# Batch 0's keys and queries of head pairs 2 and 3 transposed at their landing, ahead of the scores and values of pair 1

## The chip, the cores and the metric

The kernel runs on one core of one Trainium2 chip. Times are device microseconds (us) of that core. Runs of the kernel before differ by 0.4 to 0.9 us within one set of rounds; for each comparison the kernel before was run on the same chip in the same rounds. All runs here count as fast in the sense of the run's state. The *granted clock* is the share of full TensorE clock that the throttle granted, averaged over a run or a stretch. A load *lands* when its transfer is complete. A profiled span is 1.8 us shorter than the time of the same run.

## The reference, cut to what matters

Chunked attention over 4 batches, 8 heads, 768 positions, 64 wide: each chunk of 32 queries sees 16 positions to its left, 8 to its right and 8 memory slots. Its output goes through a two-layer block with a sine:

```python
scores = scale * np.matmul(q_c, k_full.transpose(0, 1, 3, 2))
a = softmax(scores)                       # cut: with the maximum taken off
out[:, :, c_start:c_end] = np.matmul(a, v_full)
# ...
h = x @ w_in                              # 3072 x 512 by 512 x 2048
s = np.sin(alpha * h)
g = h + s * s / (alpha + 1e-09)
return g @ w_out
```

## The kernel before: the parts that matter

Batch 0's attention runs alone, before the first layer has anything to do. Eight *units* are worked off: unit u is head pair u // 2 and four of its eight query blocks. The order of the pieces is written by hand: k and q transpose a pair's keys or queries (TensorE) and evict them (DVE for keys, ACT for queries, DVE for pair 1's queries), s makes a unit's scores, e its exponentials on ACT, v its values, x the transposes of its output, z n multiplies zeros n times so that TensorE stays busy.

```python
ORDER = (
    "k 0,q 0,memk 0,memv 0,k 1,s 0,e 0,z 1,s 1,e 1,q 1,s 2,e 2,v 0,s 3,e 3,k 2,x 0,q 2,v 1,s 4,e 4,k 3,x 1,q 3,"
    "s 5,e 5,v 2,z 1,s 6,e 6,x 2,v 3,z 1,s 7,e 7,x 3,z 1,v 4,z 1,v 5,x 4,z 1,v 6,x 5,z 1,v 7,x 6,z 1,x 7"
)
# ... accumulators: "big" has three of two banks, "sm" two of one bank
big = ctx.enter_context(tc.tile_pool(name="big", bufs=3, space=bass.MemoryType.PSUM))
smp = ctx.enter_context(tc.tile_pool(name="smp", bufs=2, space=bass.MemoryType.PSUM))
# ... the loads of batch 0, in the order in which they are asked for
load_qk_pair(0, 0, *kq)
masks.make_identity(nc, ident[:])
load_qk_pair(0, 1, *kq)
load_v(0, 0, 16)
for hp in range(2, HP):
    load_qk_pair(0, hp, *kq)
# ... in turn(), the transposes of one pair
            spin(3 if hp < 2 else 2, z)           # fillers in front of them
# ... in exps()
                nc.scalar.activation(pt[...], sc[...], ACTF.Exp, bias=..., scale=0.125)   # cut
# ... in pv() and xt()
        ot = big.tile([P, 2, 512], F32, name="ot", tag="big")     # values of a unit
        nc.vector.reciprocal(rv, otv[0:QW, :, :, D])
        nc.vector.tensor_tensor(out=x_blk[...], in0=otv[...], in1=rv[...], op=ALU.mult)   # cut
```

The softmax here doesn't subtract the row's maximum and nothing guards it: scores larger than these inputs give would overflow.

## Time and profile before

| | |
|---|---|
| time, median | 234.26 us (233.97 to 234.29) |
| profiled span | 232.5 us |
| first layer starts | 28.00 us |
| rest of the span behind that | 204.5 us |

Only the 28 us of batch 0's attention are reordered. A start of layer one that is x us earlier is worth x us, if the other 204.5 us keep their length. The lines are in the prediction.

### The profile page before, as it was taken

To read this page: it belongs to the slowest core of one execution; us is meant where nothing else is said; L and a number is where in the kernel's file an instruction comes from. 1 tells how busy PE (TensorE), PEld (TensorE's weight loads), DVE (VectorE), ACT (ScalarE), POOL (GpSimd) and SP (SyncE) were. 2 spreads that over 40 slices of the span, in tenths; PEclk is the share of its full clock that TensorE was granted. 3 is DMA by queue.
4 is the path that set the end of the run, shared out by engine and by line. 5 is a ranking of instruction groups with operands and counts; after the bars stand their busy time and mean duration, and the time that the engine had idled before them with its cause. 6 is when DMAs were issued, how large, how long until landed. Compare 5 with 4: busy or idle time off the path is not lost.

```text
span 232.5 us, 4584 instructions
## 1 busy us (share of the span) xinstructions
PE 218.9 (94%) x1834; PEld 122.1 (53%) x1834; DVE 160.2 (69%) x287; ACT 153.0 (66%) x247; POOL 69.8 (30%) x80
## 2 busy tenths in 40 slices
PE   7978899999999999999999999998999999899994
PEld 2444555555446565654555656564555555453453
DVE  5776679898657887988467798887565458775110
ACT  3388779984797397898564877878664676880110
POOL 8898202595912115157300315020000020110000
PEclk9999999999999999999999999999999999999999
DMA  6999999999999910109993101010111010101112
GB/s 88 142 173 169 207 204 206 207 139 99 138 239 164 91 45 0 43 8 174 171 156 80 45 0 48 0 45 3 45 48 53 37 49 0 45 1 48 69 67 90
DMA packets 51805, 21.13 MB, mean 91 GB/s; under 512 B 36296, under 2 KB 48840, under 8 KB 51784
## 3 DMA queue, kind: packets, MB, share of 16 engines
q0 software_dynamic: 45568, 14.41, 70.3%
q1 hardware_dynamic: 6216, 6.43, 9.2%
q8 instruction: 14, 0.23, 0.5%
q14 instruction: 7, 0.06, 0.1%
HBM read 28.94 MB, written 6.29 MB: 152 GB/s over the span
## 4 chain that ended last, share of the span: by engine, by line
PE 66%; ACT 11%; DVE 11%; issue 5%; DMA 3%; POOL 2%; POOLq 1%; DVEq 0%; ACTq 0%
PE o L472 28%; PE hT L393 21%; DVE gT L422 5%; ACT u L405 4%; PE ot L301 3%; PE sc L270 3%; DMA k_bf<-in_k_dram 3%; ACT pt L286 2%; PE ot L316 2%; DVE x_blk L306 2%; DVE s L414 2%; ACT s L408 2%; PE tt_a L242 2%; PE o L461 2%; PE z L162 1%
## 5 line engine op out<-in xcount | busy, mean ns | idle before, releaser
L472 PE MATMUL o<-w_out_sb,gT 128*128 128x512 bf16 x336 | 90.0, 380 | 0.4 <-DVE gT L422 0.4
L393 PE MATMUL hT<-xT,w_in_sb 128*128 128x384 bf16 x488 | 87.1, 326 | 2.9 <-DVE gT L422 2.8
L422 DVE SCALAR_TENSOR_TENSOR gT<-s,inv_alpha,hT 128x768 bf16<-128x768 f32 x61 | 61.0, 1012 | 19.7 <-ACT s L408 11.6
L405 ACT ACTIVATE u<-hT,alpha_sb 128x768 f32<-128x768 f32 x61 | 54.7, 897 | 23.9 <-PE hT L393 22.9
L393 PEld LDWEIGHTS <-w_in_sb 128*128 128x128 bf16 x512 | 49.3, 98 | 37.5 <-issue 3.8
L286 ACT ACTIVATE pt<-sc,biasm 128x256 bf16<-128x256 f32 (+2 forms) x104 | 39.0, 471 | 14.6 <-PE sc L270 14.6
L472 PEld LDWEIGHTS <-gT 128*128 128x128 bf16 x336 | 29.3, 98 | 24.3 <-DVE gT L422 1.2
L410 POOL TENSOR_TENSOR s<-u 128x768 f32<-128x768 f32 x9 | 13.2, 1465 | 88.2 <-ACT u L405 61.3
L408 ACT ACTIVATE s<-u 128x768 f32<-128x768 f32 x32 | 27.0, 843 | 1.0
L414 DVE TENSOR_TENSOR s<-u 128x768 f32<-128x768 f32 x23 | 24.3, 1056 | 3.1 <-ACT u L405 3.0
L306 DVE TENSOR_TENSOR x_blk<-ot,rinv 96x512 bf16<-96x512 f32 x32 | 22.0, 686 | 1.1
L139 POOL DMA_DIRECT2D vw<-in_v_dram x24 | 22.0, 938 | 0.0
L216 POOL COPY pr<-q_bf 128x768 bf16<-128x768 bf16 x12 | 10.7, 895 | 35.7 <-PE tt_a L242 25.0
L430 DVE COPY o_sb<-o 128x512 f32<-128x512 f32 x12 | 8.3, 689 | 15.6 <-PE o L472 15.5
L430 ACT COPY o_sb<-o 128x512 f32<-128x512 f32 x11 | 6.4, 582 | 17.9 <-PE o L472 17.9
L305 DVE RECIPROCAL rinv<-ot 96x8 f32<-96x8 f32 x32 | 6.5, 202 | 16.2 <-PE ot L301 15.8
L301 PEld LDWEIGHTS <-pt 128*128 128x128 bf16 x256 | 11.8, 97 | 6.4 <-issue 1.5
L270 PEld LDWEIGHTS <-kTi 64*128 64x128 bf16 x256 | 6.9, 94 | 13.3 <-issue 6.0
L301 PE MATMUL ot<-vw,pt 128*128 128x65 bf16 x256 | 13.0, 193 | 0.6 <-ACT pt L286 0.6
L270 PE MATMUL sc<-qT,kTi 64*128 64x96 bf16 x256 | 11.2, 205 | 2.4 <-DVE qT L263 1.1
L242 PEld LDWEIGHTS <-pr 128*128 128x128 bf16 x144 | 10.0, 98 | 5.9 <-DVE pr L216 0.9
L316 PE MATMUL ot<-ident,x_blk 96*128 96x96 bf16 x128 | 10.8, 206 | 2.0 <-DVE x_blk L306 2.0
(74 smaller groups left out, 168.1 us busy)
## 6 DMA issues: line engine op xcount, KB each, us to landing
out_dram<-o_sb SPq DMA_DIRECT2D x23, 256.0 KB, 2.0
k_bf<-in_k_dram POOLq DMA_DIRECT2D x3, 768.0 KB, 7.4
q_bf<-in_q_dram POOLq DMA_DIRECT2D x3, 768.0 KB, 12.0
vw<-in_v_dram POOLq DMA_DIRECT2D x6, 384.0 KB, 14.1
w_in_sb<-in_moe_w_in_dram POOLq DMA_DIRECT2D x4, 512.0 KB, 10.1
w_out_sb<-in_moe_w_out_dram POOLq DMA_DIRECT2D x2, 1024.0 KB, 24.5
k_bf<-in_k_dram POOLq DMA_DIRECT2D x4, 192.0 KB, 5.4
q_bf<-in_q_dram POOLq DMA_DIRECT2D x4, 192.0 KB, 5.5
```

What stands on the lines that cost most here:

```text
L139: nc.gpsimd.dma_start(dst, src)
L270: nc.tensor.matmul(sc[:, e, QW * c:QW * c + QW], kTi[64 * e:64 * e + 64, hp, 104 * j:104 * j + P], qT[64 * e:64 * e + 64, hp, QW * j:QW * ...
L286: nc.scalar.activation(pt[:, 0:H * QW].rearrange("p (g e c) -> p e g c", g=4, e=2)[:, :, c0:c1, 32 * m:32 * m + 32], sc[:, :, 0:4 * QW].re ...
L301: nc.tensor.matmul(otv[:, n // 4, n % 4, :], pt[:, QW * n:QW * n + P], vws[b % 2][:, 2 * hp + n % 2, j, 0:D + 1])
L306: nc.vector.tensor_tensor(out=x_blk[:].rearrange("p (g e) d -> p g e d", g=2), in0=otv[0:QW, :, :, 0:D], in1=rv.unsqueeze(3).to_broadcast( ...
L316: nc.tensor.transpose(xtp[:, kt, :], x_blk[:, 2 * kt:2 * kt + 2, :].rearrange("p e d -> p (e d)"), ident[0:QW, 0:QW])
L393: nc.tensor.matmul(hts[hf][:, 0:HALF], w_in_sb[:, kt, P * ft:P * ft + P], xT[:, kt, HALF * hf:HALF * hf + HALF], start=(kt == 0), stop=(kt ...
L405: nc.scalar.activation(u[:], hT[:, :, 0:HALF], ACTF.Sin, scale=alpha_sb[:, ft:ft + 1])
L408: nc.scalar.activation(s2[:], u[:], ACTF.Square)
L414: nc.vector.tensor_tensor(out=s2[:], in0=u[:], in1=u[:], op=ALU.mult)
L422: nc.vector.scalar_tensor_tensor(out=gv, in0=s2[:], scalar=inv_alpha[:, ft:ft + 1], in1=hT[:, :, 0:HALF], op0=ALU.mult, op1=ALU.add)
L472: nc.tensor.matmul(o[:], gT[:, ft, P * s:P * s + P], w_out_sb[:, ft, :], start=(ft == 0), stop=(ft == FT - 1),)
```

## The change

Its intent: pairs 2 and 3 are transposed as soon as their loads land, so that ACT need not wait for them later. The fillers ahead of the four turns become 3, 3, 1, 1 and no longer 2 each.

```diff
-    "k 0,q 0,memk 0,memv 0,k 1,s 0,e 0,z 1,s 1,e 1,q 1,s 2,e 2,v 0,s 3,e 3,k 2,x 0,q 2,v 1,s 4,e 4,k 3,x 1,q 3,"
+    "k 0,q 0,memk 0,memv 0,k 1,s 0,e 0,z 1,s 1,e 1,q 1,k 2,s 2,e 2,s 3,v 0,q 2,e 3,k 3,x 0,v 1,q 3,s 4,e 4,x 1,"
     "s 5,e 5,v 2,z 1,s 6,e 6,x 2,v 3,z 1,s 7,e 7,x 3,z 1,v 4,z 1,v 5,x 4,z 1,v 6,x 5,z 1,v 7,x 6,z 1,x 7"
@@
-            spin(3 if hp < 2 else 2, z)
+            spin(3 if hp < 2 else (3 - 2 * (hp - 2)), z)
```

## The prediction

> **What bounds the kernel now.** The span by stage comes first. This is the table of busy times in four stretches; the columns are the stretch in us, its length, the busy time and instruction count of PE, PEld, DVE, ACT and POOL, the granted clock, the DMA share and GB/s.
>
> ```profile
> 10.00:14.00 4.00, 2.94 (x59) 1.71 (x56) 2.83 (x6) 2.98 (x10) 4.00 (x6) 1.00 1.51 187
> 14.00:20.00 6.00, 5.46 (x97) 3.13 (x94) 4.45 (x12) 4.56 (x13) 6.00 (x9) 1.00 2.33 150
> 20.00:28.00 8.00, 5.80 (x98) 3.78 (x97) 6.12 (x16) 7.15 (x18) 3.98 (x5) 1.00 1.29 200
> 28.00:52.00 24.00, 22.98 (x144) 13.41 (x142) 19.82 (x23) 20.59 (x28) 10.27 (x10) 1.00 1.31 190
> ```
>
> The change edits only the order of batch 0's attention, which runs up to 28.0 us; the other 204.5 us keep their instructions and their order. So the change can be worth only what it takes off the moment at which the first layer's matmuls start. In 20 to 28 us ACT is the busiest (7.15 of 8.00); in 14 to 20 us ACT is busy for 4.56 of 6.00 and PE for 5.46, but part of the latter is the filler multiplications of zeros. The next view, ACT in order of time, shows where ACT stood still. "pt<-sc" is the exponentials of units of four cells, four instructions each; "qT<-z" is the eviction of a pair's transposed queries.
>
> ```profile
> 10.41 2.60 ACT L286 ACTIVATE pt<-sc,biasm 128x64 bf16<-128x64 f32 x8 [1.46 <-PE sc L270]
> 13.62 2.60 ACT L286 ACTIVATE pt<-sc,biasm 128x64 bf16<-128x64 f32 x8 [0.61 <-PE sc L270]
> 16.40 0.80 ACT L263 COPY qT<-z 128x768 bf16<-128x768 bf16 x1 [0.19 <-PE z L245]
> 17.64 1.35 ACT L286 ACTIVATE pt<-sc,biasm 128x64 bf16<-128x64 f32 x4 [0.44 <-PE sc L270]
> 19.80 0.80 ACT L263 COPY qT<-z 128x768 bf16<-128x768 bf16 x1 [0.81 <-PE z L245]
> 20.50 3.85 ACT L286 ACTIVATE pt<-sc,biasm 128x256 bf16<-128x256 f32 x12
> 24.36 1.28 ACT L369 ACT_TABLE_LOAD   x1
> ```
>
> Units 2 and 3 run from 13.62, unit 4 at 17.64, units 5 to 7 from 20.50 without a gap. Between 13.62 and 20.50 ACT stood idle for 0.19 + 0.44 + 0.81 = 1.44 us, each time for something made from the keys or queries of pairs 2 and 3, which were transposed late. The chain of work that ended last says that this idle time is paid for (start, duration, what):
>
> ```profile
> 18.87 0.43 PE z L162 x2
> 19.30 0.47 PE z L245 x12
> 19.80 0.80 ACT qT L263
> 20.60 1.26 ACT pt L286 x4
> 21.86 0.04 issue
> 21.91 0.42 PE ot L301 x8
> 22.32 0.02 issue
> 22.35 0.21 DVE rinv L305
> ```
>
> It goes from the transposes of pair 3's queries (19.30) through their eviction and unit 5's exponentials to unit 3's values at 21.91. Those values do not use unit 5: its exponentials hold the two-bank accumulator that unit 3's values are given, as the code's three "big" buffers in rotation show (unit 5's scores, then unit 3's values, take the same one). After 22 us the chain alternates DVE, PE and ACT to the start of layer one at 28.0.
>
> The last view is the issue of pair 2's keys, size and time from the start of issue to landing; ahead of it the queue's own line, with its start.
>
> ```profile
> 7.51 0.78 POOL L107 DMA_DIRECT2D k_bf<-in_k_dram  x1
> ```
> ```profile
> k_bf<-in_k_dram POOLq DMA_DIRECT2D x1, 192.0 KB, 5.5
> ```
>
> So pair 2's keys land at 7.51 + 5.5 = 13.0. From the same two views for the others: pair 2's queries 8.25 + 5.8 = 14.05, pair 3's keys 9.81 + 5.2 = 15.0, its queries 10.89 + 5.2 = 16.1. The kernel before transposes these at 14.67, 15.84, 18.07 and 19.23: up to 3 us after landing.
>
> **What the Trainium skill says.** "PSUM — Partial Sum Buffer", section "Engine vs sequencer instructions", calls the queues of ScalarE and VectorE strict FIFO and says that matmuls start and complete in program order. The trace agrees: the transposes of unit 0's output start at 15.13 and take 0.34, but their DVE copy starts at 16.24, behind pair 2's key copies (15.24 to 16.24). So an eviction put forward delays what stood ahead of it. "TensorE: Matmul & The Clock Gate", section "Step-by-step: what each phase is for", says that only weight loads are pulled ahead; here one weight load for unit 4's scores ran at 16.64 while its matmul waited until 17.25. So keys put in front of unit 2's scores can hold those scores, by their DMA too. "ScalarE: Activation LUTs", section "What ACT_TABLE_LOAD costs", gives about 1283 ns and a drain of 1380 ns; the load here took 1.28 us and the sine after it began at 25.66, so no such drain is seen. This load follows unit 7's exponentials and moves with them.
>
> **The change part by part.** No instruction is added or removed. Four evictions (two of 1.00 us of DVE for keys with their edges, two of 0.80 us of ACT) and 48 transposes move forward. The filler was 2 multiplications in front of each of four turns (8); it is 3, 3, 1, 1 (8). I replay the order with durations of the traced rows, as steps from one start to the next: 12 transposes 0.46 on PE (0.53 to their end), a unit's scores 0.28 and values 0.35, fillers 0.75 for three and 0.31 for one, exponentials 1.30 to 1.33, reciprocal 0.24, scaling 0.69, DVE copy of an output block 0.32; 0.04 for a hand-over.
>
> Up to the transposes of pair 1's queries (11.65 to 12.18) nothing differs.
> - *Pair 2's keys.* Three fillers end at 12.86, landing is 13.0: transposes 13.03 to 13.56. PE was waiting for the DVE copy of pair 1's queries until 13.18 anyway, so most of this is in idle time.
> - *Units 2 and 3's scores, unit 0's values.* Scores 2 at 13.49, against 13.23: 0.26 lost. Exponentials 2 run 13.88 to 15.18. Scores 3 at 13.77, values 0 at 14.05 to 14.47.
> - *DVE.* Pair 2's key copies 13.60 to 14.60, then unit 0's reciprocal and scaling to 15.53, against 14.89.
> - *Pair 2's queries.* Three fillers from 14.40, transposes 15.15 to 15.68, eviction on ACT 15.71 to 16.51. ACT waits 0.53 for it, from 15.18, because it stands in front of exponentials 3. These then run 16.51 to 17.81, against an end at 16.22.
> - *Pair 3's keys, unit 0's transposes, unit 1's values, pair 3's queries.* Keys 15.92 to 16.45; output transposes 16.38; values 1 at 16.56; one filler 16.91; queries 17.22 to 17.75. Their eviction finds ACT just free: 17.81 to 18.61.
> - *From there ACT is never idle.* Exponentials 4 run 18.61 to 19.94 (before: 17.64 to 18.99, so later); 5 to 21.26 (before 21.86), 6 to 22.55, 7 to 23.84 (before 24.35). DVE meanwhile copies pair 3's keys (16.49 to 17.49) and output 0, scales unit 1 by 18.74; output 1 is transposed at 18.78, scores 5 at 19.06, values 2 at 19.53, scores 6 at 20.18, output 2 at 20.96. All are earlier than before by 0.4 or more, or ready for ACT in time.
> - *Values 3* get their buffer at 21.26 and start at 21.31 instead of 21.91: 0.60 gained. After that the chain is the same as before. Output 4's copy waits for ACT's table load and sine; both move with unit 7's end, by 0.51.
>
> The sum, checked on ACT: idle time falls from 1.44 to 0.53 (0.91 gained), unit 2 starts 0.26 later, and about 0.1 is lost as hand-overs that overlapped: 0.5 to 0.6. Layer one starts at about 27.45. Nothing behind it should eat this: in 28 to 60 us no wait for a DMA is listed among the waits, the first quarter of the first weights lands at 17.39 + 6.7 = 24.1, and the output weights issued at 22.88 and 23.75 land at 45.3 and 50.4, the first 5 us ahead of their first use at 50.40. The second is used only after the first two accumulators' first halves.
>
> **The rivals.** First, *the moved work costs more than it frees*: DVE and ACT are FIFO, and pair 3's queries reach ACT with 0.06 us of slack only. Against it stands that each landing is ahead of its transposes except pair 2's keys. If those landed at 13.6 instead of 13.0, everything to unit 7 would move by up to 0.6 and the time would be 234.2. Second, *the gain is hidden*: the end of the stage has its own bound of DVE, PE and ACT hand-overs, busy 6.12 of 8.00 us on DVE. For it speaks that unit 4's end becomes later (19.94); against it that the chain named unit 5's exponentials as what released unit 3's values. It would give 234.2 too. Third, *a larger gain*: if PE runs its fillers and transposes faster than my steps, pair 2's queries reach ACT by 15.2, the wait of 0.53 vanishes and about 1.0 us is saved: 233.2. Against it stands that the steps are read off this same trace. Fourth, *a longer stage*: with evictions ahead of unit 0's and 1's scaling, the values of pair 1 could be held by the accumulators so that PE idles and ACT drains; I would expect 234.8. The values of pairs 2 and 3 landing at 20.0 to 22.1 do not forbid the earlier values 4 at 23.14.
>
> **Range and chances.** 234.26 - 0.55 = 233.7 us. The replay may be off by some 0.5 us in either direction (one landing, one hand-over on ACT), and the runs of before spread over 0.3: 233.0 to 234.4 should hold it 8 times in 10. Two per cent is 4.7 us; all ACT idle time in the whole reordered stretch is 1.44, so faster by over 2% is 1%, within 2% is 98%, and slower by over 2%, which would need a new wait that repeats beyond this stage, is 1%.
>
> **What would show it.** Right: scores 2 about 0.26 later behind the landing of pair 2's keys; ACT without a gap from the eviction of pair 2's queries (about 15.7) to the table load, which starts near 23.84; exponentials 4 later and 5 earlier than before; values 3 near 21.3; layer one near 27.45; all later stages shifted by one constant. Wrong: an ACT gap in front of pair 3's query eviction, values 3 still at 21.9 with another releaser, or the shift at 28 us gone by 52 us.

## The result, and the profile after

The changed kernel took 233.72 us in the median of four runs (233.18 to 234.03), the kernel before 234.12 (233.91 to 234.29). Ratios here are the mean time of one kernel's fast runs over that of the other's of the same rounds, so not quite the ratio of the medians. This one is 0.9981, with a 95% interval of 0.9957 to 1.0005. The size is near the predicted one; the interval still holds 1.

ACT after, in order of time, to be laid beside ACT before in the prediction:

```profile
15.20 0.80 ACT L263 COPY qT<-z 128x768 bf16<-128x768 bf16 x1 [0.27 <-PE z L245]
15.89 1.36 ACT L286 ACTIVATE pt<-sc,biasm 128x256 bf16<-128x256 f32 x4
...
17.86 3.85 ACT L286 ACTIVATE pt<-sc,biasm 128x64 bf16<-128x64 f32 x12
22.38 1.35 ACT L286 ACTIVATE pt<-sc,biasm 128x256 bf16<-128x256 f32 x4 [0.67 <-PE sc L270]
23.75 1.28 ACT L369 ACT_TABLE_LOAD   x1
```

Units 4 to 6 now run without a gap from 17.86, before 4 began at 17.64 and 5 only at 20.50. The two gaps that stood ahead of units 4 and 5 are gone. But unit 7 waited 0.67 us for its scores, which nobody had foreseen. PE after, around that time:

```profile
12.73 0.53 PE L245 MATMUL z<-ident,k_bf 128*64 128x128 bf16 x12 [0.27 <-DMA k_bf<-in_k_dram]
...
19.27 0.40 PE L301 MATMUL ot<-vw,pt 128*128 128x65 bf16 x8 [0.43 <-ACT pt L286]
...
20.87 0.60 PE L301 MATMUL ot<-vw,pt 128*128 128x65 bf16 x8
21.28 0.62 PE L162 MATMUL z<-zeros 128*128 128x512 bf16 x1
...
27.55 0.34 PE L316 MATMUL ot<-ident,x_blk 96*128 96x96 bf16 x4 [0.28 <-DVE x_blk L306]
```

Unit 3's values start at 20.87, 1.04 us earlier than the 21.91 of before. The last output transposes start at 27.55 (layer one at 27.73) against 27.82 before: of the 1.04, only 0.27 is left. In between the same eight value matmuls took 0.60 instead of 0.40, a filler 0.62 instead of 0.38. The busy times by stretch say why (columns as in the prediction; the third value from the end is the granted clock). First the changed kernel, then the kernel before:

```profile
20.00:22.00 2.00, 1.47 (x27) 0.86 (x23) 1.44 (x4) 1.71 (x6) 1.55 (x3) 0.73 1.36 186
22.00:24.00 2.00, 1.84 (x22) 1.16 (x19) 0.90 (x3) 1.60 (x5) 2.00 (x3) 0.50 1.26 212
24.00:26.00 2.00, 1.69 (x27) 1.25 (x26) 1.83 (x6) 1.71 (x3) 0.16 (x1) 0.92 1.23 202
```
```profile
20.00:22.00 2.00, 1.39 (x27) 0.91 (x26) 1.10 (x3) 2.00 (x7) 1.35 (x2) 1.00 1.44 179
22.00:24.00 2.00, 1.47 (x31) 0.97 (x31) 1.33 (x4) 2.00 (x8) 1.98 (x3) 1.00 1.25 207
```

The changed kernel ran at half clock for about 3.4 us, from 20.9 to 24.3, as stretches of half a us show. From 28 us on the two traces run in parallel: the first output matmul starts at 50.40 before and at 50.13 after, again 0.27 apart. So two things are mixed in the 0.4 us, a gain from the order and a loss from the clock. A third one, the landing of pair 2's keys, is in the first line above: PE waited for it, and it came at 7.51 + 5.2 = 12.7 here, where the trace before had promised 13.0.

### The profile page after: what moved, and what is told of

Its sections match the earlier page's. It is cut to its first block, busy times and chain, and to the rows that moved or that the text cites. A ratio compares the mean times of both kernels' runs of the same rounds, so it can differ in the third digit from the quotient of the medians.

```text
span 232.2 us, 4583 instructions
## 1 busy us (share of the span) xinstructions
PE 219.2 (94%) x1834; PEld 122.7 (53%) x1834; DVE 160.1 (69%) x287; ACT 153.0 (66%) x247; POOL 70.0 (30%) x80
## 4 chain that ended last, share of the span: by engine, by line
PE 64%; ACT 12%; DVE 11%; issue 5%; POOL 3%; DMA 2%; POOLq 1%; DVEq 0%; ACTq 0%
PE o L472 28%; PE hT L393 21%; DVE gT L422 5%; ACT u L405 4%; PE ot L301 3%; ACT pt L286 3%; PE sc L270 3%; DVE x_blk L306 2%; PE ot L316 2%; DMA k_bf<-in_k_dram 2%; DVE s L414 2%; ACT s L408 2%; PE tt_a L242 2%; PE o L461 2%; PE o L442 1%
## 5 line engine op out<-in xcount | busy, mean ns | idle before, releaser
L286 ACT ACTIVATE pt<-sc,biasm 128x256 bf16<-128x256 f32 (+2 forms) x104 | 39.1, 470 | 15.1 <-PE sc L270 15.1
L472 PEld LDWEIGHTS <-gT 128*128 128x128 bf16 x336 | 29.3, 98 | 24.3 <-DVE gT L422 1.2
L414 DVE TENSOR_TENSOR s<-u 128x768 f32<-128x768 f32 x23 | 24.3, 1056 | 3.1 <-ACT u L405 3.0
L301 PEld LDWEIGHTS <-pt 128*128 128x128 bf16 x256 | 12.4, 100 | 6.7 <-issue 2.2
L301 PE MATMUL ot<-vw,pt 128*128 128x65 bf16 x256 | 13.6, 197 | 0.9 <-ACT pt L286 0.9
L316 PEld LDWEIGHTS <-x_blk 96*128 96x128 bf16 x128 | 8.3, 98 | 8.4 <-DVE x_blk L306 3.8
```

The costliest lines, as they stand in the source:

```text
L286: nc.scalar.activation(pt[:, 0:H * QW].rearrange("p (g e c) -> p e g c", g=4, e=2)[:, :, c0:c1, 32 * m:32 * m + 32], sc[:, :, 0:4 * QW].re ...
L301: nc.tensor.matmul(otv[:, n // 4, n % 4, :], pt[:, QW * n:QW * n + P], vws[b % 2][:, 2 * hp + n % 2, j, 0:D + 1])
L316: nc.tensor.transpose(xtp[:, kt, :], x_blk[:, 2 * kt:2 * kt + 2, :].rearrange("p e d -> p (e d)"), ident[0:QW, 0:QW])
L414: nc.vector.tensor_tensor(out=s2[:], in0=u[:], in1=u[:], op=ALU.mult)
L472: nc.tensor.matmul(o[:], gT[:, ft, P * s:P * s + P], w_out_sb[:, ft, :], start=(ft == 0), stop=(ft == FT - 1),)
```

## The experiments

My theory by now: (1) ACT's idle time from unit 2 on sets the start of layer one; (2) the new order hangs on the landing of pair 2's keys, which varies; (3) the new order leaves TensorE so thinly busy from 17 to 21 us that the clock sometimes drops. The rivals: the filler split carries the gain; the end of the stage is set by hand-overs between PE and DVE; the clock drop is an accident that belongs to any order. All outputs are right.

To compare traces whose loads landed at different times I use one distance throughout: from the start of unit 2's scores to the start of layer one. It was 14.77 us before (13.23 to 28.00):

```profile
9.56 0.53 PE L245 MATMUL zb<-ident,k_bf 128*64 128x128 bf16 x12 [0.51 <-DMA k_bf<-in_k_dram]
...
13.23 0.34 PE L270 MATMUL sc<-qT,kTi 64*128 64x96 bf16 x8 [1.06 <-DVE qT L263]
...
28.00 1.30 PE L393 MATMUL hT<-xT,w_in_sb 128*128 128x384 bf16 x7
```

This distance leaves out what the landing of pair 2's keys costs ahead of it. For that, a second one starts at the transposes of pair 1's keys (9.56), which stand ahead of everything that was reordered: 28.00 - 9.56 = 18.44 before.

### The changed kernel again

No edit.

> The changed kernel once more, unaltered, for a second trace. Ordering theory: the ratio to the kernel before is again about 0.998 (0.3 to 0.6 us gained). Clock theory (the traced run of the changed kernel had a slower granted clock, about 0.79 in 20 to 28 us, and paid some 0.7 us for it): if the drop is the rule for this order, this trace shows it again, with unit 3's values about 1.0 us earlier than before but layer one only 0.3 earlier; if it was chance, the clock is 1.00 in 20 to 28 us and layer one starts 0.8 or more earlier than before (27.2 or less).

Six runs: 233.00 to 235.47 us, median 233.61, before 233.87 (11 runs). The ratio was 1.0007 (0.9976 to 1.0037): in this round no gain at all in the mean. The runs split by their clock. The four with a mean clock of 0.998 or more took 233.00, 233.05, 233.15 and 234.07; the two with 0.992 and 0.985 took 234.42 and 235.47. The traced run had full clock:

```profile
8.61 0.53 PE L245 MATMUL zb<-ident,k_bf 128*64 128x128 bf16 x12 [0.19 <-DMA k_bf<-in_k_dram]
...
12.35 0.53 PE L245 MATMUL z<-ident,k_bf 128*64 128x128 bf16 x12 [0.37 <-DMA k_bf<-in_k_dram]
12.80 0.51 PE L270 MATMUL sc<-qT,kTi 64*128 64x96 bf16 x16
...
19.02 0.40 PE L301 MATMUL ot<-vw,pt 128*128 128x65 bf16 x8 [0.43 <-ACT pt L286]
...
26.75 2.44 PE L393 MATMUL hT<-xT,w_in_sb 128*128 128x384 bf16 x14
```

The distance is 26.75 - 12.80 = 13.95, against 14.54 in the first trace (13.19 to 27.73): the clock drop cost 0.6 us there. The order alone is worth 14.77 - 13.95 = 0.82, less what scores 2 are held by the landing. They came 4.19 us after pair 1's keys and not 3.67 as before, so 0.52 goes back: from pair 1's keys to layer one it is 18.14 here, 0.30 less than before.

### Fillers as before, in the new order

```diff
-            spin(3 if hp < 2 else (3 - 2 * (hp - 2)), z)
+            spin(3 if hp < 2 else 2, z)
```

> New order, but the fillers as before: 2 in front of each of the four turns, not 3, 3, 1, 1. Ordering theory: pair 2's keys wait for their landing anyway, pair 2's queries reach ACT about 0.2 us earlier, pair 3's queries after that no later in ACT's row; time within 0.2 us of the changed kernel. Rival (the filler split carries the gain): the gain falls below 0.2 us.

Median 233.24 us, ratio 0.9977 (0.9959 to 0.9995). The traced distance is 13.63 (12.94 to 26.57), 0.32 shorter than with 3, 3, 1, 1. Against the changed kernel of the same rounds its median is 0.37 lower; within 0.2 had been expected. Its ACT, then its PE lines for unit 2's values and for layer one:

```profile
17.14 0.80 ACT L263 COPY qT<-z 128x768 bf16<-128x768 bf16 x1 [0.35 <-PE z L245]
...
22.94 1.28 ACT L369 ACT_TABLE_LOAD   x1
```

```profile
18.76 0.40 PE L301 MATMUL ot<-vw,pt 128*128 128x65 bf16 x8 [0.17 <-DVE xT L319]
...
26.57 2.60 PE L393 MATMUL hT<-xT,w_in_sb 128*128 128x384 bf16 x15
```

Unit 2's values wait here for the DVE copy of output 1. In the changed kernel they waited for ACT, until unit 4's exponentials ended. The waits in the two compiled programs say the same: the first matmul of these values waits for DVE in one and for ACT in the other, and unit 6's scores the other way round. So the accumulators are not given out in strict rotation; the change of fillers alone altered which one unit 2's values got, and it was the worse one. The filler split carries no gain: with it the path is 0.32 us longer. How much of this is the accumulator and how much the fillers themselves was not separated.

### The new fillers alone, in the old order

```diff
-            spin(3 if hp < 2 else 2, z)
+            spin(3 if hp < 2 else (3 - 2 * (hp - 2)), z)
```

> Old order with the new filler split (3 in front of each of pair 2's turns, 1 in front of pair 3's). Ordering theory: nothing gained, 0.995 to 1.003 of before, perhaps 0.2 us lost on pair 2's queries and won back on pair 3's, which were on the path. Rival (the fillers carry it): 0.3 to 0.6 us gained here already.

Ratio 1.0003 (0.9989 to 1.0017), traced distance 14.77 (13.01 to 27.78), as before. The rival falls.

### The gaps of PE filled

```diff
-    "... v 1,q 3,s 4,e 4,x 1,"
-    "s 5,e 5,v 2,z 1,s 6,e 6,x 2,v 3, ..."
+    "... v 1,q 3,s 4,e 4,z 2,x 1,"
+    "s 5,e 5,z 1,v 2,z 1,s 6,e 6,z 2,x 2,v 3, ..."
```

> The changed kernel with five more multiplications of zeros, put where its trace showed PE waiting between 17.6 and 20.7 us (two ahead of unit 1's output transposes, one ahead of unit 2's values, two ahead of unit 2's output transposes). Clock theory: the granted clock stays 1.00 in 20 to 28 us, layer one starts 0.4 us or more earlier than in the traced changed kernel (27.3 or less) and the time is 0.3 to 0.7 us below the changed kernel's slower runs, about 233.2. Ordering theory alone (the clock is an accident that costs nothing on the path): the same time as the changed kernel or slightly more for the added work.

No run had a mean clock under 0.998. But the median was 234.11 us, ratio 1.0009 (0.9993 to 1.0026): the expected time was missed by 0.9. Its trace shows where that run lost it:

```profile
13.85 0.53 PE L245 MATMUL z<-ident,k_bf 128*64 128x128 bf16 x12 [1.00 <-DMA k_bf<-in_k_dram]
```

Pair 2's keys landed at 13.8, 1.5 us later than in the second trace of the changed kernel, and PE waited 1.00 for them. The distance from scores 2 on is 13.80 (14.31 to 28.11), so the fillers did not lengthen the path in this trace. The load is the same program in both; in this traced run it took 6.3 us from issue to landing, in the others 4.8 to 5.6. Why all six runs of this kernel were slowish (mean 234.09, where the changed kernel's four at full clock had 233.32 in the same rounds) was not traced and stays open.

### Pair 2's keys asked for earlier

```diff
     load_qk_pair(0, 1, *kq)
+    load_qk_one(k, kq[0], 2)      # pair 2's keys
     load_v(0, 0, 16)
-    for hp in range(2, HP):
-        load_qk_pair(0, hp, *kq)
+    load_qk_one(q, kq[1], 2)
+    load_qk_pair(0, 3, *kq)
```

> The changed kernel with one load moved: pair 2's keys are asked for ahead of unit 0's and 1's values instead of behind them. So far the traces of the new order agree that layer one starts a fixed 14.1 to 14.4 us after pair 2's keys are transposed (12.35 to 26.75, 12.48 to 26.57, 13.85 to 28.11; 12.73 to 27.73 with a clock drop), so their landing, 12.3 to 13.8, would set the end of the stage. Landing theory: PE no longer waits for that DMA, scores 2 start when pair 1's queries are copied, layer one starts at 26.2 to 27.0 and the runs without a clock drop are at 232.6 to 233.1. Rival (the stage's end is set elsewhere and the fixed distance is chance): layer one stays at 26.6 to 28, times as the changed kernel's. Second rival: the values of unit 0, now 0.7 us later in the queue, become the wait.

PE no longer waits for the DMA:

```profile
12.66 0.53 PE L252 MATMUL z<-ident,k_bf 128*64 128x128 bf16 x12
...
27.14 2.12 PE L400 MATMUL hT<-xT,w_in_sb 128*128 128x384 bf16 x12
```

But the gain was not what I expected: layer one at 27.14, not 26.2 to 27.0, and 233.09, 233.36 and 233.45 us in the three runs at full clock, as the changed kernel. Scores 2, at 13.20, now wait for the DVE copy of pair 1's queries (12.19 to 13.14), and pair 1's keys are transposed at 9.37, later than the 8.6 to 9.1 of the first three traces of the new order. That the moved load made them late is not shown: with all loads in their old places they came at 9.49 in the trace with gaps filled, and with this load moved at 8.83 in the trace with the gaps filled as well. Counted from them, scores 2 came after 3.83 us, where the new order with the old loads has 4.10 to 4.82, and layer one after 17.77, where the changed kernel had 18.14. So this trace gained about 0.4 us behind pair 1's keys and lost more than that ahead of them. The last stretch, from the end of the exponentials to layer one, is 3.89 here. Three of six runs had clocks of 0.993, 0.983 and 0.978 and took 234.11, 234.91 and 235.82, which makes the ratio 1.0013 (0.998 to 1.0046).

### The same load moved, in the old order

> The old order with the same load moved. There pair 2's keys are transposed at 14.67, long after landing, and layer one started 18.44 us after pair 1's keys were transposed in both traces at hand. Landing theory: nothing gained, 0.998 to 1.003 of before, and the distance of 18.44 from pair 1's keys stands. Rival (an earlier key load speeds either order, by the queue): 0.3 us or more gained here too.

The distance is 14.76, and 18.43 from pair 1's keys, both as expected. The time was worse than expected: ratio 1.0034 (1.0013 to 1.0055), with one of four runs at a clock of 0.991. The profiled run, 234.33, has the 232.5 of the traced kernel before as its span, but it too lies above the 233.95 of before in these rounds. Why all four runs were slower is open.

### Both: keys earlier and gaps filled

> The same load moved, with the five fillers in PE's waits of 17.6 to 20.7 us as well. Clock theory: so far the mean granted clock was 0.993 or less in 5 of 16 runs of the new order, and in none of the runs of before, of the old order with new fillers, or of the new order with its gaps filled; here too no run falls below 0.997, and the spread of the times is under 0.8 us, all at 232.6 to 233.3. Rival (the five fillers themselves slow the stage, as the six slow runs of the gaps-filled kernel could also be read): 0.5 us or more above the kernel with only the load moved.

No run under 0.998, median 233.73 us, ratio 0.999 (0.9974 to 1.0006). The clock part held, the times did not: 233.14 to 234.35, wider and later than 232.6 to 233.3. The mean, 233.71, is 0.41 above the three runs at full clock of the kernel with only the load moved, near the 0.5 of the rival (the fillers themselves slow the stage). In its trace the distance is 14.18, pair 2's queries reached ACT 0.43 us late, and the values of unit 4 waited 0.21 us for a load of values. So this rival is not ruled out here.

### Pair 2's keys asked for later

The mirror image, in the kernel with two fillers everywhere: pair 2's queries are asked for first.

```diff
-    for hp in range(2, HP):
-        load_qk_pair(0, hp, *kq)
+    load_qk_one(q, kq[1], 2)
+    load_qk_one(k, kq[0], 2)
+    load_qk_pair(0, 3, *kq)
```

> The new order with two fillers everywhere, and pair 2's queries asked for ahead of its keys instead of behind them: the keys land about 0.75 us later, nothing else in the queue moves. Landing theory: PE waits for the keys 0.7 us longer than the 0.52 of the kernel with two fillers (1.2 or so), scores 2 start 0.7 us later after pair 1's keys are transposed (4.13 becomes 4.8), the distance from scores 2 to layer one stays at 13.6, and the runs without a clock drop take 233.4 to 234.0 and not 232.7 to 233.3. Rival (the landing is hidden, as it would be in the old order): scores 2 and the time as with two fillers.

Median 234.59 us, ratio 1.002 (1.0005 to 1.0035); the five runs at full clock took 234.12 to 234.87. The traced keys landed at 8.25 + 5.7 = 13.95 and PE waited:

```profile
14.02 0.53 PE L252 MATMUL z<-ident,k_bf 128*64 128x128 bf16 x12 [1.86 <-DMA k_bf<-in_k_dram]
```

From pair 1's keys to scores 2 it took 5.46 (9.02 to 14.48) instead of 4.13: 1.33 us, where I had expected 0.7. The traced run then fell to half clock (0.61 in 14 to 18 us), so its distance of 15.10 says nothing. The times say it: the five runs at full clock have a mean of 234.47, the eight of the kernel with two fillers (two sets of rounds, one below) 233.33, so 1.1 us of the 1.33 is paid; set against the kernel before of the same rounds it is 1.1 too (0.45 slower, 0.66 faster). This load lies on the path of the new order. In the old order, by its first trace, there were 1.7 us between landing and use (13.0 to 14.67).

### Pair 3's query eviction done twice

```diff
         t = turn(qb, hp)
+        if qb.shape[1] != 6 and hp == 3:
+            copy(qT[:, hp, :]..., t[...])      # the same eviction once more
         copy(qT[:, hp, :]..., t[...])
```

> The changed kernel with pair 3's query eviction done twice on ACT (0.80 us more of ACT ahead of unit 4's exponentials, same result). By the prediction ACT is the row without gaps that ends the stage: layer one 0.7 us later after pair 2's keys than the 14.1 to 14.4 us of the new order, so 14.8 to 15.1. Rival (from unit 2's values on, the end is set by hand-overs between PE and DVE and ACT has slack): less than 0.3 us later, 14.1 to 14.6.

From pair 2's keys to layer one it took 14.71 (12.64 to 27.35), between the expected 14.8 to 15.1 and the rival's 14.1 to 14.6, so by its own terms this test does not decide. The distance from scores 2 is 14.25: 0.30 more than in the changed kernel, 0.62 more than with two fillers everywhere. The second comparison is the fair one: in this build unit 2's values got the DVE-freed accumulator, as there. Its ACT:

```profile
17.08 0.80 ACT L264 COPY qT<-z 128x768 bf16<-128x768 bf16 x1
17.91 0.80 ACT L265 COPY qT<-z 128x768 bf16<-128x768 bf16 x1
18.60 5.09 ACT L288 ACTIVATE pt<-sc,biasm 128x64 bf16<-128x64 f32 x16
23.71 1.28 ACT L371 ACT_TABLE_LOAD   x1
```

The second eviction adds 0.83 us from start to start (17.08 to 17.91). The first begins 3.98 us after scores 2, 0.22 earlier than with two fillers (12.94 to 17.14), and the end moved by 0.62. What is added on ACT comes out at the end, so ACT sets the end. The time: median 234.42 us, ratio 1.0022 (0.9996 to 1.0047), with one of four runs at a clock of 0.993. The same is seen without any doubling: from the table load, that is the end of the exponentials, to layer one it takes 3.62 to 3.64 us in eight traces, old and new order alike (24.36 to 28.00 before, 22.94 to 26.57 with two fillers, 23.71 to 27.35 here). In the changed kernel at full clock it is 3.75, where unit 7 waits for its scores, and 3.89 and 3.90 in the two new-order kernels with the earlier key load; there the end is not ACT's alone.

### Only pair 2 moved

```diff
-    "... q 1,k 2,s 2,e 2,s 3,v 0,q 2,e 3,k 3,x 0,v 1,q 3,s 4,e 4,x 1,"
+    "... q 1,k 2,s 2,e 2,s 3,v 0,q 2,e 3,x 0,v 1,s 4,e 4,k 3,x 1,q 3,"
```
(with two fillers everywhere)

> One part alone: only pair 2's keys and queries are moved forward; pair 3's stay behind unit 4's exponentials as before, two fillers everywhere. By the prediction ACT then waits for pair 3's queries again: ACT idle of 0.3 to 0.8 us ahead of that eviction, and scores 2 to layer one between the old 14.77 and the new 13.6, near 14.2. Rival (pair 2 alone carries the gain): 13.6 to 13.8. Second rival (pair 3 alone): 14.7 or more.

The distance is 13.63 (13.67 to 27.30), the same as with both pairs moved. The rival was right: pair 2 alone carries the whole gain. ACT:

```profile
16.16 2.60 ACT L286 ACTIVATE pt<-sc,biasm 128x256 bf16<-128x256 f32 x8
19.10 0.80 ACT L263 COPY qT<-z 128x768 bf16<-128x768 bf16 x1 [0.34 <-PE z L245]
19.80 3.85 ACT L286 ACTIVATE pt<-sc,biasm 128x256 bf16<-128x256 f32 x12
23.66 1.28 ACT L369 ACT_TABLE_LOAD   x1
```

ACT idles 0.34 us ahead of pair 3's queries, now behind unit 4. With both pairs moved and the same fillers it idles 0.35 ahead of the same eviction, only earlier, behind unit 3. The sum of ACT's idle time behind unit 2's start is the same, and so is the end. Moving pair 2 brings scores 4 forward (2.89 us after scores 2 instead of 4.02), and pair 3 follows in its old place. Moving pair 3 as well buys nothing. Median 233.76 us, ratio 0.998 (0.9965 to 0.9995), though PE waited 1.17 for the keys in this trace; none of its six runs was under 0.998 in clock.

### Two fillers everywhere, with and without the gaps filled

> The new order with two fillers everywhere, a second time beside the one with gaps filled. Expected: scores 2 to layer one again 13.6, runs without a clock drop 232.7 to 233.4, one or two of six runs with a mean clock near 0.993 and 0.6 us or more slower. If no run drops and the times equal those of the other, the clock is not what separates fast from slow runs.

> New order, fillers 2 in front of every turn as before, and the five fillers in PE's waits: meant to beat both kernels. In the traces so far layer one starts 14.77 us after scores 2 in the old order and 13.95 in the changed kernel, but 13.63 with two fillers everywhere, because unit 2's values then take the buffer that output 1's copy frees and not the one that unit 4's exponentials hold. Buffer and clock theory: 13.6 to 13.8 here, no run with a mean clock under 0.997, 0.996 to 0.998 of before with all runs between 232.7 and 233.6. Rival (the added fillers cost more than the clock drops): at or above the kernel without them, 0.998 to 1.000.

With the gaps filled: median 233.17 us (232.82 to 233.72), before 234.17, ratio 0.9965 (0.9951 to 0.998). It is the fastest kernel of the study and clear of the kernel before. The distance was 13.64. One run, 233.72, lies above the range that I gave. Without the gaps filled: median 233.83, ratio 0.9984 (0.9969 to 0.9999), two of six runs at a clock of 0.993 (233.87 and 233.88). A slow one, 234.22, had full clock, so the clock is not the only thing that parts slow from fast runs; of the four at full clock only one (233.08) lies in the expected 232.7 to 233.4. The traced run of the kernel without was one with a drop; its distance is 14.23 (13.36 to 27.59) and not 13.63, again 0.6 us. Without, then with the gaps filled:

```profile
18.00:21.00 3.00, 1.91 (x37) 1.34 (x38) 1.59 (x5) 3.00 (x11) 3.00 (x5) 1.00 1.87 148
21.00:24.00 3.00, 2.83 (x33) 1.63 (x33) 1.82 (x6) 2.88 (x9) 3.00 (x4) 0.53 1.24 207
```
```profile
18.00:21.00 3.00, 2.94 (x46) 1.68 (x45) 1.59 (x5) 3.00 (x12) 2.92 (x5) 1.00 2.13 148
21.00:24.00 3.00, 1.91 (x36) 1.17 (x33) 2.38 (x7) 2.98 (x8) 2.31 (x4) 1.00 1.26 207
```

PE was busy for 1.91 of 3.00 us ahead of the drop, and for 2.94 where no drop came. Yet the second kernel was at 1.91 later on, without a drop, and from 17 to 21 us the second trace of the changed kernel was at 2.19 of 4.00 without one, while the two with a drop were at 2.29 and 2.70 (before 3.69). So a thin stretch does not force a drop. Over all runs, with a mean clock of 0.993 or less counted as a drop:

| order | runs | with a drop |
|---|---|---|
| old (before in the four rounds with known clocks, new fillers, keys earlier) | 54 | 1 |
| new, gaps not filled (five kernels in seven rounds) | 38 | 12 |
| new, only pair 2 moved | 6 | 0 |
| new, gaps filled (three kernels) | 18 | 0 |

The rival that a drop belongs to any order falls. In 54 runs the old order had one drop. If the fillers in the gaps did nothing, 12 drops and none would fall out like this about once in 200 times; the 6 runs of pair 2 alone (PE busy for 3.54 of 4.00 from 17 to 21 us) are too few to say the same. One stretch of 3.4 us at half clock takes 0.007 from the mean of 232 us, so 0.993 is one drop, as in both traces, and 0.985 and 0.978 would be two and three (an estimate; not traced).

Against their counterparts in the same rounds the three kernels with gaps filled were 0.23 us slower, 0.41 faster and 0.48 faster in the mean of all runs; against the counterparts' runs at full clock, 0.77 and 0.41 slower and 0.40 faster. So the fillers go with the absence of drops; a gain in time by both measures is seen only with two fillers everywhere, and there the intervals of the two ratios still overlap (0.9951 to 0.998, 0.9969 to 0.9999).

One thing is open in all these comparisons. In the three traces of the old order pair 1's keys were transposed at 9.34 to 9.62, in the eleven of the new one at 8.61 to 9.49, though nothing ahead of them was changed. Whether that is chance was not tested; part of the gain in time may be due to it. Counted from there, layer one came after 18.43 to 18.44 us in the old order and after 17.76 and 17.77 with two fillers at full clock, 18.14 in the changed kernel, 18.40 with only pair 2 moved and 18.62 with the changed kernel's gaps filled. Scores 2 came after 4.13, 4.13, 4.19, 4.77 and 4.82 in these five, for 3.67 in the old order: in a single trace the landing can take back most of what the order gains.

## Why the prediction was right, point by point

**The time.** 233.7 was predicted, 233.72 measured. That it fits so closely is luck: none of the four runs lies nearer than 0.28 us to their median, one had a clock drop, and the kernel before was 0.14 faster than in the prediction. The mean of all ten runs of the changed kernel is 233.78, hardly under the mean of before in the same rounds (233.93). Without the three runs that had a drop the mean is 233.42: 0.5 us gained, near the predicted 0.55, though two of these seven took 234.03 and 234.07. The predicted mechanism is there, and its size fits behind scores 2 (0.82 in the trace, 0.81 predicted); the clock, which no step and no rival named, gives most of it back in the mean.

**The bound.** That "this idle time is paid for" was right, and it is shown: more ACT work moved the end, and the distance from the end of the exponentials to layer one is 3.6 us before and with two fillers, 3.75 in the changed kernel. Between the old order and the new one with two fillers, the idle time behind unit 2's start falls from 1.44 to about 0.35 and the distance by 1.14.

**The replay.** It gave 13.49 for scores 2 and 27.45 for layer one, a distance of 13.96; the trace at full clock has 13.95. Exponentials 4 later and 5 earlier than before, as said. Values 3 were predicted 7.82 us after scores 2 and came 7.83 after them (12.80 to 20.63). Two of its terms were off and cancelled. The table load came 10.20 us after scores 2 and not 10.35, because PE reached pair 2's queries sooner than in the replay: the wait for them was 0.27 and not 0.53. Layer one came 3.75 after the table load and not 3.61. And "ACT is never idle" from there was wrong: unit 7 waited 0.16 for its scores at full clock, and 0.67 behind the drop.

**Pair 2's keys.** That scores 2 would be held by this landing was right in kind and in sign (0.27 to 1.17 us of waiting in the traces of the new order with the loads in their old places). The landing itself, taken as 13.0 from one trace, was 12.3 to 13.8: the working gave it too little spread. Its cost was taken as 0.26; counted from pair 1's keys scores 2 came 0.43 to 1.15 later than before. In the trace of the changed kernel at full clock it was 0.52, which leaves 0.30 of the 0.82. This is the term that was too small.

**The buffers.** The step of the three buffers "in rotation" held in the kernel before for the two users that it named. In the changed one unit 2's values took the accumulator of unit 4's scores, which the replay did not have. With two fillers everywhere they got another, and the path was 0.32 us shorter.

**What the parts are worth.** The part by part account moved all four evictions and did not ask which were needed. Pair 2 alone would have given the whole gain. Moving pair 3 too only moves ACT's wait of 0.35 us from behind unit 4 to behind unit 3.

**The rivals.** The second, that the end hides the gain, falls: the drop-free distance is shorter by 0.82. The third, a larger gain of 1.0 us, came half true in its cause: PE was faster than the steps, and half of the wait of 0.53 was gone. With two fillers everywhere all of it was gone (1.14 gained behind scores 2), and with the gaps filled as well the ratio of 0.9965 is 0.8 us. The first, a late landing, came true in the traces of variants; the changed kernel's own runs of 234.03 and 234.07 at full clock were not traced. The fourth, values held by the accumulators, was right in kind for unit 2's values, at 0.3 us and not the 0.5 or more that it gave. "All later stages shifted by one constant" holds: the span behind the start of layer one was 204.4 to 204.6 us in every trace.

## What to carry to other kernels

On a hand-ordered path, find the engine whose idle time reaches the end, and move only what removes that idle time: here one pair did it all, and the second one bought nothing. Moving a consumer up to its load's landing puts that load's scatter on the path, so ask how widely landings vary, from more than one trace. And look at the granted clock of every run: a gain of 0.5 us is easily paid back by 3.4 us at half clock, and no drop was seen in the 18 runs that had a few multiplications of zeros in the waits, though only one of these three kernels was then faster than its counterpart at full clock.

## What the Trainium skill lacked or had wrong

- "TensorE: Matmul & The Clock Gate", section "Why this matters for your kernels", advises against idle gaps of TensorE over about 3 us. Here the clock halved with no gap over 0.6 us: TensorE was busy for 1.91 of the 3.00 us ahead of the drop. The section "A second HAM failure mode: psum-queue depth-cycling" does name frequent short idle times as a cause, but no share of busy time; 2.94 of 3.00 was seen in one of the three kernels that had no drop in 18 runs, and 1.91 of 3.00 was also seen without one.
- The same page, section "What's actually happening", gives half rate and a free-running window of about 3.4 us. The traces agree on rate and length: 0.50 of the clock, for about 3.4 us (20.9 to 24.3 in one trace, 21.2 to 24.6 in another). That the window runs free they do not show; by their mean clocks 12 of 38 runs of the same kind of order had a drop and 26 had none.
- "ScalarE: Activation LUTs", section "What ACT_TABLE_LOAD costs", adds a drain of 1380 ns to the load. The load took 1.28 us here and the next activation began 0.02 us after it.
- No page says how widely the landing of one load varies from run to run. The same load of 192 KB, in the same place of the queue, took 4.8 to 6.3 us from issue to landing in the traces.
